# A self-scheduling kernel: longer assumed waits and a fixed seed in its planner, late buffers moved from VectorE to ScalarE, new filler rules, and query stores assumed to land later

## The chip, the cores and the metric

The kernel runs on one core of a Trainium2 chip. A core has TensorE (PE; its weight loads are listed as PEld), VectorE (DVE), ScalarE (ACT), GpSimd (POOL) and SyncE (SP, which issues most transfers here). The metric is the time of one execution in microseconds of device time, as a median of several runs. A span (first to last instruction of a profiled execution) is about 1.8 us shorter than the timed run.

## The reference

Two independent blocks over 2048 rows of width 640, their outputs side by side:

```python
# A: a diagonal complex state-space layer
h[t] = Lam_bar * h[t-1] + B_bar @ x[t]
y[t] = 2 * Re(C @ h[t]) + Dskip * x[t]
# B: attention with 32 heads of 20, one shared key and value head, no mask
q = (x @ wq) split into 32 heads;  k = x @ wk;  v = x @ wv
p = softmax(q k^T / sqrt(20));     out = concat(p v) @ wo
```

The attention makes 32 x 2048 x 2048 scores. The kernel cuts them into 2048 tiles of 128 x 512, and each needs an exponential.

## The kernel before

The kernel does not state an order of instructions. A small event-driven scheduler, which runs while the kernel is built, is given steps with assumed durations and priorities and picks, engine by engine, what goes next. What it picks is emitted as five fixed instruction streams with the semaphore waits that the data needs. The durations in it are assumptions; on the chip only the order counts.

Most score tiles have their exponential on ScalarE, two or three at a time out of a slot of PSUM banks. The others go to VectorE, which makes an approximation by integer arithmetic on the bits of a bf16 (a first pass, then three shifted copies, which GpSimd shares). How many go to VectorE is bounded by `SHARE`, but is decided by what is free at the moment:

```python
OUT = {"pe": 200.0, "act": 130.0, "dve": 110.0, "pool": 150.0, "dma": 60.0}   # ns until a result is seen elsewhere
...
def fill(self, op, i):                       # one ScalarE slot: scores of 2 or 3 tiles, then the exponential
    ...
    ex = self.act(lambda e: e.activation(dst, t[:, 0:512 * n], ACT.Exp, scale=1.0 / UNIT),
                  0.8333 * 512 * n + 64, table="exp", deps=[op], ...)
...
def want_d(self, taken=0, own=0):            # may a tile go to VectorE?
    if self.tile_n >= NTILE - self.LAST or self.d_count + taken + own + 1 > self.SHARE * (self.tile_n - 16):
        return False
    if len(self.d_banks()) <= taken or self.behind():
        return False
    return len(self.d_free()) > taken + own + len(self.SHIFTS) - 1
...
def planned(self):                           # before: the best of 24 seeds by the plan's own end
    for seed in range(self.PLANS):
        ...
        end = max(op.end for op in plan.s.order)
```

The seed moves the due times of background tasks (projections, the state-space layer, output products) by a few tiles, so each seed gives another order, and also another number of tiles on VectorE. Filler products multiply zeros on TensorE and are meant to keep its clock up (in the trace of before it was halved for 6.83 us after 3.41 us in which TensorE was busy for 2.40; that fillers prevent this is not shown by itself in any run here): one source before the first value product (`warm_source`), another after it (`keep_source`).

Of the kernel before, what the change touches and what calls it, by code (L numbers as in the profile page):

```python
# [22 lines left out]
class Op:  # L23


    __slots__ = ("eng", "fns", "dur", "deps", "prio", "reads", "writes", "prev", "gate", "hook", "start", "end",
                 "seq", "land", "dma_key", "idx", "tail", "mode", "load", "late", "port", "after", "due", "table", "psum")

    def __init__(self, eng, fns, dur, deps=(), prio=5, reads=(), writes=(), prev=None, gate=None, hook=None,
                 dma_key=None, land=0.0, tail=0.0, mode="F", load=0.0, port=False):  # L30
        self.eng, self.fns, self.dur = eng, list(fns), dur
        self.deps, self.prio, self.prev = list(deps), prio, prev
        self.reads, self.writes = list(reads), list(writes)
        self.gate, self.hook = gate, hook
        self.dma_key, self.land, self.tail = dma_key, land, tail
        self.mode, self.load, self.late = mode, load, False
        self.port, self.after, self.due, self.table = port, [], None, None
        self.psum = any(k[0] == "B" and k[1:].isdigit() for k in self.reads)
        self.start = self.end = None
        self.seq = self.idx = 0  # L40


class Schedule:
# [5 lines left out]
    ENGINES = ("pe", "act", "dve", "pool", "sp")  # L49
    OUT = {"pe": 200.0, "act": 130.0, "dve": 110.0, "pool": 150.0, "dma": 60.0}  # L50
    OWN = {"pe": 0.0, "act": 60.0, "dve": 115.0, "pool": 100.0}
# [10 lines left out]
    def __init__(self, seed=0):  # L62
# [16 lines left out]
        self.port_wanted = False  # L79
        self.pipe, self.table = 0.0, None  # L80

    def recent(self, span):
# [45 lines left out]
    def begin(self, op, eng):  # L128
# [5 lines left out]
        if eng == "pe":  # L134
            if op.mode != self.mode:
                op.dur += self.SWITCH
                self.mode = op.mode
            self.loads.append((self.t, op.load))
        if op.port:
            if eng == "pool" and self.port_last["dve"] is not None:  # L140
                op.after.append(self.port_last["dve"])
            self.port_free[eng] = self.t + op.dur + (self.LOCK if eng == "pool" else 0.0)
            self.port_last[eng] = op
            self.at(self.port_free[eng])
        if op.dma_key is not None:
            self.free[eng] = self.t + op.tail * len(op.fns)
            s = max(self.t + 1300.0, self.dma_free.get(eng, 0.0), self.pipe)
            self.dma_free[eng] = self.pipe = s + op.dur
# [8 lines left out]
        self.at(self.free[eng])  # L157
        for lag in (0.0, 60.0, 100.0, 110.0, 115.0, 130.0, 150.0, 200.0):
            self.at(op.end + lag)

    stay = staticmethod(lambda: True)
# [244 lines left out]
S, D, NC, H, DH = 2048, 640, 5, 32, 20  # L406
# [8 lines left out]
class Build:  # L415
# [5 lines left out]
    NDS = 20  # L421
    MORE = 21
    SHARE = 0.265
# [15 lines left out]
    def build(self):  # L439
        nc = self.nc  # L440
        with ExitStack() as o:
# [10 lines left out]
            with ExitStack() as p2:  # L452
# [11 lines left out]
                shares.update({f"CT{tb}_{c}": [f"xn{tb}"] for tb in range(2) for c in range(NC)})  # L464
                shares.update({f"DR{self.NDS + i}": over for i, over in enumerate(self.dr_over)})
                shares["WOt"] = [f"BT{i}_{c}" for i in range(2) for c in range(NC)]
                shares.update({f"OPT{k}": [f"BA{i}_{c}" for i in range(2) for c in range(NC)] for k in self.EARLY_O})
# [20 lines left out]

    SPREAD = 12.0
    PLANS = 24  # L490

    def planned(self):

        best = None
        for seed in range(self.PLANS):
            plan = copy.copy(self)
            plan.s = Schedule(seed)
            plan.program()
            try:
                plan.s.run()  # L500
            except RuntimeError:
                continue
            end = max(op.end for op in plan.s.order)
            if best is None or end < best[0]:
# [3 lines left out]
    def alloc(self, o):  # L508
# [9 lines left out]
        for c in range(NC):  # L518
            for m in range(2):
                self.dr_at.append(2048 * c + 640 + 512 * m)  # L520
                self.dr_over.append([f"xbT{i}_{c}" for i in (1, 2, 3)])
        for m in range(6):
            self.dr_at.append(ends[0] + 512 * m)
            self.dr_over.append(["wqa", "wqb"])
        for m in range(NC):
            self.dr_at.append(ends[1] + 512 * m)
            self.dr_over.append([f"QP{m}"])
        self.xaT = sb(o, "xaT", [128, NC, 2, 512], BF16)
# [126 lines left out]
    def program(self):  # L655
# [11 lines left out]
        self.state_op = {}  # L667
        self.owner = [None] * self.NPT
        self.pr_at = 0
# [30 lines left out]
    def warm_source(self):  # L700
# [4 lines left out]
        if self.started:  # L705
            if self.s.recent(3000.0) > self.WARM:
                return None
            fns = self.four(self.pvbank, [p.VZ[:]] * 4, p.KT[:, 0:512], True, True)
            return Op("pe", fns, self.mmt(512), prio=3.5, mode="C", load=512.0, reads=["VZ", "KT0"], writes=[self.pvbank.key],
                      deps=[self.c_op["VZ"], self.kt_op[0]])  # L710
        return Op("pe", [self.mm(self.pvbank.ap, p.PR[:, 0, 0:128], p.PR[:, 0, :], True, True)], 260.0, prio=9,
                  load=512.0, deps=[self.zero_op], reads=["PR0"], writes=[self.pvbank.key], hook=self.warm_last)

    WARM = 4500.0
    V_AT, BOUND_AT = (-88, -87), -99


    KEEP = 3500.0

    def keep_source(self):  # L720
# [6 lines left out]
        if self.s.recent(3000.0) > self.KEEP:  # L727
            return None
        p = self
        bank = self.pvbank  # L730
# [249 lines left out]
    def bound_task(self, m, bank):  # L980
# [3 lines left out]
        for blk in range(NC):  # L984
            prev = self.pe([lambda e, blk=blk: e.matmul(bank.cols(blk, blk + 1), lhsT=p.pick[:, 128 * blk:128 * blk + 128],
                                                        rhs=p.mab[0:DH, 4:5], start=True, stop=True)], 250.0, mode="F", load=8.0,
                           deps=[m, self.c_op["pick"]] + bank.last, prev=prev, prio=1.5, reads=["pick", "mabs"], writes=[bank.key])
        col = bass.AP(tensor=bank.tensor, offset=bank.off, ap=[[bank.tensor.shape[1], 128], [1, NC], [0, 32]])
# [43 lines left out]
    def q_task(self, qb, blk, bank):  # L1032
# [3 lines left out]
        for c in range(NC):  # L1036
# [7 lines left out]
        out = self.dma(lambda e: e.dma_start(rows, dst), 131072, f"qd{blk}", deps=[ev], reads=[key], writes=[f"qd{qb}_{blk}"], prio=0,  # L1044
                       land=300.0)
        self.qd_op[qb, blk] = out
# [137 lines left out]
    def fill(self, op, i):  # L1184
# [17 lines left out]
        for x, m in enumerate(tiles):  # L1202
            b, kc, j = self.score(op, m, t[:, 512 * x:512 * x + 512], banks[x])
            ents.append((b, kc, j, p.PR[:, h.index + x, :]))
        first = [] if own is None else [self.fill_d(op, own, banks[2])]
# [10 lines left out]
        op.load = 128.0 * len(op.fns)  # L1216
        dst = p.PR[:, h.index:h.index + n, :]
        ex = self.act(lambda e: e.activation(dst, t[:, 0:512 * n], ACT.Exp, scale=1.0 / UNIT),  # L1218
# [36 lines left out]
    def pr_next(self, n):  # L1255
        return self.pr_at if self.pr_at + n <= self.NPT else 0

# [173 lines left out]
    def more(self):  # L1431

        yield lambda: NQB - 1 in self.row_mm and self.s.done([self.row_mm[NQB - 1]]) \
            and all(self.s.done([self.qd_op[NQB - 1, i]]) for i in range(NC))
        self.dhold += [Holder(self.NDS + i) for i in range(self.MORE)]

    def d_free(self):
# [866 lines left out]
```

## Time and profile before

| | before |
|---|---|
| median of 3 runs | 745.29 us (744.67 to 746.3) |
| span of the profiled run | 743.5 us |
| ScalarE busy | 97% |
| first exponential starts, last ends | 23.0, 734.4 us |
| exponentials of 1024 and of 1536 columns | 475, 201 |
| score tiles on ScalarE, on VectorE | 1553, 495 |

An exponential over 1024 columns is two tiles, one over 1536 is three. The prediction shows the lines themselves. Read the group rows with care: in "busy, mean ns | idle before" the mean is that of single records, and the records of successive exponentials overlap: in this profile one over 1024 columns has a mean of 1112 ns, and ends 917 ns after the one before it.

### The profile page before, as it was taken

The page shows a single profiled execution, that of the slowest core. Times are in us where ns is not written, and L with a number is a line of the kernel's source. Part 1 is how long each engine was busy: PE and PEld are TensorE (multiplying, and loading weights), DVE is VectorE, ACT ScalarE, POOL GpSimd, SP SyncE. Part 2 cuts the span into 40 slices and gives each one's busy share as a digit, 9 for nine tenths or more (in the row PEclk, how much of TensorE's full clock was granted, in tenths as well). Part 3 has the DMA queues.
Part 4 walks back from the last instruction along what each step waited for, and adds up shares of the span by engine and source line. Part 5 has one row for each costly group of instructions (what it writes and reads, how often), then busy time and mean ns, then how long its engine had stood idle before and what let it go on. Part 6 is the DMA issues. An engine that isn't in the chain of part 4 may idle for free.

```text
span 743.5 us, 26647 instructions
## 1 busy us (share of the span) xinstructions
PE 711.7 (96%) x11323; PEld 255.9 (34%) x11323; DVE 665.3 (89%) x1367; ACT 722.9 (97%) x702; POOL 426.3 (57%) x448
## 2 busy tenths in 40 slices
PE   9999899998999999999999999989999999999997
PEld 3422222234443533332333333323333333332332
DVE  6888999989788798999898999998998998988995
ACT  5999999999999999999999999999999999999995
POOL 3766566430266558367476674566754835778460
PEclk9999999999999999999999999998999999999999
DMA  9414443364220100101100000110000011100101
GB/s 200 70 41 129 91 113 90 89 144 78 48 60 10 25 20 21 51 11 35 42 26 23 17 30 19 40 46 19 19 14 19 9 27 30 37 16 17 26 14 37
DMA packets 78089, 34.43 MB, mean 46 GB/s; under 512 B 58852, under 2 KB 77972, under 8 KB 77972
## 3 DMA queue, kind: packets, MB, share of 16 engines
q1 hardware_dynamic: 76352, 32.34, 18.3%
q8 instruction: 90, 1.47, 0.8%
q10 hardware_dynamic: 1620, 0.39, 0.3%
q14 instruction: 27, 0.22, 0.1%
HBM read 11.53 MB, written 9.75 MB: 29 GB/s over the span
## 4 chain that ended last, share of the span: by engine, by line
ACT 59%; PE 34%; DVE 6%; issue 1%; DVEq 0%
ACT PR L1218 59%; PE MB L637 12%; PE SC L637 11%; PE MB L633 10%; DVE BIG L652 2%; DVE prod L647 1%; DVE W L652 1%; DVE CT L647 1%; DVE CA L647 1%; DVE g L2046 0%; PE SC L633 0%; DVE pvsb L1580 0%; DVE CT L651 0%; DVE CA L651 0%; PE SC L935 0%
## 5 line engine op out<-in xcount | busy, mean ns | idle before, releaser
L1218 ACT ACTIVATE PR<-SC 128x1024 bf16<-128x1024 f32 (+1 forms) x676 | 708.6, 1252 | 3.3 <-PE SC L637 2.1
L647 POOL TENSOR_TENSOR BIG<-BIG,step 128x512 int32<-128x512 int32 x401 | 407.4, 1045 | 286.1 <-DVE BIG L652 163.1
L652 DVE TENSOR_SCALAR BIG<-SC 128x512 int16<-128x512 f32 x456 | 302.8, 684 | 38.5 <-PE SC L637 34.9
L637 PE MATMUL SC<-QT,KT 32*128 32x512 bf16 x2009 | 265.3, 386 | 23.0 <-ACT PR L1218 16.0
L637 PE MATMUL MB<-BIG,VS 128*32 128x512 bf16 x1980 | 248.5, 386 | 1.2 <-issue 0.6
L637 PE MATMUL MB<-PR,VP 128*32 128x512 bf16 x1553 | 217.4, 386 | 0.8 <-DVE pvsb L1580 0.6
L637 PEld LDWEIGHTS SC<-QT,KT 32*128 32x128 bf16 x2009 | 67.8, 91 | 258.2 <-ACT PR L1218 165.3
L652 DVE TENSOR_SCALAR BIG<-BIG 128x1024 int16<-128x1024 int16 (+1 forms) x356 | 129.0, 419 | 8.6 <-PE MB L637 7.0
L637 PEld LDWEIGHTS MB<-BIG,VS 128*32 128x32 bf16 x1980 | 62.6, 95 | 66.7 <-issue 44.1
L637 PEld LDWEIGHTS MB<-PR,VP 128*32 128x32 bf16 x1553 | 53.5, 94 | 54.6 <-issue 41.0
L633 PE MATMUL MB<-CT,W 128*32 128x320 bf16 (+2 forms) x1040 | 49.7, 301 | 0.2 <-DVE BIG L2006 0.2
L633 PE MATMUL MB<-xaT,BT 128*32 128x256 bf16 x800 | 34.5, 274 | 0.0
L633 PE MATMUL MB<-xaT,BA 128*32 128x256 bf16 x800 | 33.6, 274 | 0.1
L633 PE MATMUL MB<-CA,W 128*32 128x512 bf16 (+1 forms) x640 | 31.2, 301 | 0.1
L647 DVE TENSOR_TENSOR prod<-MB,tab 128x1024 bf16<-128x1024 f32 x20 | 24.3, 1215 | 3.7 <-PE MB L633 3.7
L652 DVE TENSOR_SCALAR BIG<-MB 128x512 int16<-128x512 f32 x39 | 26.5, 680 | 1.1 <-PE MB L637 0.7
L633 PEld LDWEIGHTS MB<-CT,W 128*32 128x32 bf16 x1040 | 21.4, 96 | 17.0 <-issue 7.9
L633 PE MATMUL MB<-WO,OP 128*32 128x128 bf16 (+1 forms) x576 | 26.5, 297 | 0.1
L1761 DVE CAST stg<-MB 128x512 bf16<-128x512 f32 x35 | 23.9, 683 | 2.6 <-PE MB L633 2.3
L633 PE MATMUL MB<-BIG 128*32 128x512 bf16 x340 | 25.6, 383 | 0.0
L2046 DVE TENSOR_TENSOR_SCAN g<-sc,hst,prod 128x256 bf16<-128x256 f32 x30 | 23.1, 776 | 0.0
L633 PEld LDWEIGHTS MB<-xaT,BA 128*32 128x32 bf16 x800 | 19.0, 96 | 9.0 <-issue 5.4
(167 smaller groups left out, 421.2 us busy)
## 6 DMA issues: line engine op xcount, KB each, us to landing
out_dram<-stg SPq DMA_DIRECT2D x31, 128.0 KB, 1.7
qd<-BIG SPq DMA_DIRECT2D x20, 128.0 KB, 1.8
QT<-qd SPq DMA_DIRECT2D x28, 80.0 KB
OP<-pvsb SPq DMA_DIRECT2D x105, 20.0 KB
rdP<-recs SPq DMA_DIRECT2D x105, 20.0 KB
W<-in_A_B_re_dram SPq DMA_DIRECT2D x10, 160.0 KB, 2.7
W<-in_A_B_im_dram SPq DMA_DIRECT2D x10, 160.0 KB, 2.7
lbd<-W SPq DMA_DIRECT2D x10, 160.0 KB, 2.0
```

What stands on the lines that cost most here:

```text
L633: r = e.matmul(out[32 * j:32 * j + 32], lhsT=lhsT[:, 32 * j:32 * j + 32], rhs=rhs, start=start, stop=stop, tile_position=(0, 32 * j), skip ...
L637: return lambda e: e.matmul(out, lhsT=lhsT, rhs=rhs, start=start, stop=stop, **kw)
L647: return lambda e: e.tensor_tensor(out, a, b, op)
L652: return lambda e: e.tensor_scalar(out, a, s1, s2, op0=op0, op1=op1)
L1218: ex = self.act(lambda e: e.activation(dst, t[:, 0:512 * n], ACT.Exp, scale=1.0 / UNIT), 0.8333 * 512 * n + 64, table="exp", deps=[op], re ...
L1761: ev = self.dve(lambda e: e.tensor_copy(st, bank.ap), 645, deps=[prev], reads=[bank.key], writes=[key], prio=self.EV, gate=(lambda: last.e ...
L2046: o = self.dve(lambda e, ri=ri, init=init: e.tensor_tensor_scan(p.g[:, u, ri, :], rdec, p.prod[:, 1, 0, ri, :], init, ALU.mult, ALU.add), ...
```

## The change

The intent, as the code reads: make the plan agree with the chip. Steps are lengthened by the waits that will be emitted, a finished plan is replayed with all of these waits and penalised for stretches of low TensorE activity, one seed that scores well is fixed, fillers become urgent when activity is low, and late buffers are shared out differently.

```diff
-    OUT = {"pe": 200.0, "act": 130.0, ...}
+    OUT = {"pe": 200.0, "act": 225.0, ...}
+    SEEN = {"pe": 215.0, "act": 225.0, ...}          # for the replay
 ...
+        wait = self.stall(op)                        # waits for all readers and writers of its buffers
+        if wait > 0.0:
+            if op.dma_key is None:
+                op.dur += wait
+                op.stall = wait
 ...
+    def replayed(self): ...                          # end of the replay + self.gated(work)
+    WINDOW, IDLE, RANGE, COST = 3413.0, 2700.0, 700.0, 1500.0
 ...
-    MORE = 21                                        # more VectorE tile buffers, late in the kernel
+    MORE = 10
 ...
-    PLANS = 24
+    SEEDS = (198,)
-            end = max(op.end for op in plan.s.order)
+            end = plan.s.replayed()
 ...
+        self.wide_at = [(self.NPT, 6, ends[0]), (self.NPT + 6, NC, ends[1])]   # 11 buffers to ScalarE instead
 ...
+            low = self.s.mode != "S" and self.s.recent(2800.0) < self.LOW
-            return Op("pe", fns, ..., prio=3.5, ...)                 # warm_source
+            return Op("pe", fns, ..., prio=0.3 if low else 2.5, ...)
-    WARM = 4500.0
+    WARM = 3500.0
 ...
+        low = self.s.mode != "S" and self.s.recent(2800.0) < self.LOW   # keep_source: computed, not used
         return Op("pe", fns, self.mmt(256, 4), prio=8, ...)
 ...
-                       land=300.0)
+                       land=4000.0 if qb > 1 else 300.0)              # query stores
```

Left out: the code of the replay, the addressing of the shared buffers, warm-up durations of 240 instead of 260 ns, the priority 0.5 instead of 1.5 of five small products that make the score bound, and the seed's spread of due times, 8 tiles instead of 12 (`SPREAD`). The constants of the score are its author's assumptions; of its clock constants only the 3413 ns has a counterpart in the traces here, the 3.41 us steps told of below.

More of the change, by code (lines that the diff above doesn't have):

```diff
@@ L26 @@
     __slots__ = ("eng", "fns", "dur", "deps", "prio", "reads", "writes", "prev", "gate", "hook", "start", "end",
-                 "seq", "land", "dma_key", "idx", "tail", "mode", "load", "late", "port", "after", "due", "table", "psum")
+                 "seq", "land", "dma_key", "idx", "tail", "mode", "load", "late", "port", "after", "due", "table", "psum", "stall", "found")
     def __init__(self, eng, fns, dur, deps=(), prio=5, reads=(), writes=(), prev=None, gate=None, hook=None,
@@ L39, in __init__ @@
         self.start = self.end = None
+        self.stall = 0.0
         self.seq = self.idx = 0
@@ L49 @@
     ENGINES = ("pe", "act", "dve", "pool", "sp")
-    OUT = {"pe": 200.0, "act": 130.0, "dve": 110.0, "pool": 150.0, "dma": 60.0}
+    OUT = {"pe": 200.0, "act": 225.0, "dve": 110.0, "pool": 150.0, "dma": 60.0}
+    SEEN = {"pe": 215.0, "act": 225.0, "dve": 110.0, "pool": 150.0, "dma": 60.0}
     OWN = {"pe": 0.0, "act": 60.0, "dve": 115.0, "pool": 100.0}
@@ L80, in __init__, with stall @@
         self.pipe, self.table = 0.0, None
+        self.writer, self.readers = {}, {}
+    def stall(self, op):
+        eng, late = op.eng, self.t
+        found = list(op.after)
+        for k in op.reads:
+            if k in self.writer:
+                found.append(self.writer[k])
+            if k[0] == "B" and k[1:].isdigit():
+                found += [x for x in self.readers.get(k, ()) if x.eng != eng]
+        for k in op.writes:
+            if k in self.writer:
+                found.append(self.writer[k])
+            found += self.readers.get(k, ())
+        op.found = [d for d in found if d is not op and (eng != "pe" or d.eng != "pe")]
+        for d in op.found:
+            late = max(late, self.seen(d, eng))
+        for k in op.reads:
+            self.readers.setdefault(k, []).append(op)
+        for k in op.writes:
+            self.writer[k] = op
+            self.readers[k] = []
+        return late - self.t
     def recent(self, span):
@@ L138, in begin @@
             self.loads.append((self.t, op.load))
+        if op.port and eng == "pool" and self.port_last["dve"] is not None:
+            op.after.append(self.port_last["dve"])
+        wait = self.stall(op)
[3 more added lines that the diff above has]
+                op.stall = wait
         if op.port:
-            if eng == "pool" and self.port_last["dve"] is not None:
-                op.after.append(self.port_last["dve"])
             self.port_free[eng] = self.t + op.dur + (self.LOCK if eng == "pool" else 0.0)
@@ L145, in begin @@
         if op.dma_key is not None:
-            self.free[eng] = self.t + op.tail * len(op.fns)
-            s = max(self.t + 1300.0, self.dma_free.get(eng, 0.0), self.pipe)
+            self.free[eng] = self.t + wait + op.tail * len(op.fns)
+            s = max(self.t + wait + 1300.0, self.dma_free.get(eng, 0.0), self.pipe)
             self.dma_free[eng] = self.pipe = s + op.dur
@@ L157, in begin, with replayed, gated @@
         self.at(self.free[eng])
-        for lag in (0.0, 60.0, 100.0, 110.0, 115.0, 130.0, 150.0, 200.0):
+        for lag in (0.0, 60.0, 100.0, 110.0, 115.0, 150.0, 200.0, 225.0):
             self.at(op.end + lag)
+    def replayed(self):
+        free = {e: 0.0 for e in self.ENGINES}
+        port = {"dve": 0.0, "pool": 0.0}
+        end, queue, work = {}, 0.0, []
+        for op in self.order:
+            e = op.eng
+            t = free[e]
+            for d in op.found:
+                out = self.SEEN["dma"] if d.dma_key is not None else self.OWN.get(e, 0.0) if d.eng == e else self.SEEN[d.eng]
+                t = max(t, end[id(d)] + out)
+            dur = op.dur - op.stall
+            if op.port:
+                t = max(t, port["pool" if e == "dve" else "dve"])
+                port[e] = t + dur + (self.LOCK if e == "pool" else 0.0)
+            if op.dma_key is not None:
+                free[e] = t + op.tail * len(op.fns)
+                queue = max(t + 1300.0, queue) + dur
+                end[id(op)] = max(queue + 700.0, free[e] + 1700.0) + op.land
+            else:
+                end[id(op)] = t + dur + op.tail
+                free[e] = t + dur - (self.EARLIER.get(e, 0.0) if op.psum else 0.0)
+                if e == "pe" and t > 14000.0:
+                    work.append((t, op.load))
+        return max(end.values()) + self.gated(work)
+    WINDOW, IDLE, RANGE, COST = 3413.0, 2700.0, 700.0, 1500.0
+    def gated(self, work):
+        low, lo, total = [], 0, 0.0
+        for t, w in work[:-40]:
+            total += w
+            while work[lo][0] < t - self.WINDOW:
+                total -= work[lo][1]
+                lo += 1
+            if total - w < self.IDLE and t - work[0][0] > self.WINDOW:
+                if low and t - low[-1][0] < 2 * self.WINDOW:
+                    low[-1][1] = min(low[-1][1], total - w)
+                else:
+                    low.append([t, total - w])
+        return sum(self.COST * min(1.0, (self.IDLE - v) / self.RANGE) for t, v in low)
     stay = staticmethod(lambda: True)
@@ L465, in build @@
                 shares.update({f"DR{self.NDS + i}": over for i, over in enumerate(self.dr_over)})
+                shares.update({f"PR{self.NPT + i}": over for i, over in enumerate(self.pr_over)})
                 shares["WOt"] = [f"BT{i}_{c}" for i in range(2) for c in range(NC)]
@@ L487, in lay_banks @@
         self.early = [b for b in self.banks if b not in rest]
-    SPREAD = 12.0
-    PLANS = 24
+    SPREAD = 8.0
+    SEEDS = (198,)
     def planned(self):
         best = None
-        for seed in range(self.PLANS):
+        for seed in self.SEEDS:
             plan = copy.copy(self)
@@ L521, in alloc @@
                 self.dr_over.append([f"xbT{i}_{c}" for i in (1, 2, 3)])
-        for m in range(6):
-            self.dr_at.append(ends[0] + 512 * m)
-            self.dr_over.append(["wqa", "wqb"])
-        for m in range(NC):
-            self.dr_at.append(ends[1] + 512 * m)
-            self.dr_over.append([f"QP{m}"])
+        self.wide_at = [(self.NPT, 6, ends[0]), (self.NPT + 6, NC, ends[1])]
+        self.pr_over = [["wqa", "wqb"]] * 6 + [[f"QP{m}"] for m in range(NC)]
         self.xaT = sb(o, "xaT", [128, NC, 2, 512], BF16)
@@ L667, in program @@
         self.state_op = {}
-        self.owner = [None] * self.NPT
+        self.owner = [None] * (self.NPT + len(self.pr_over))
+        self.wide = False
         self.pr_at = 0
@@ L707, in warm_source @@
                 return None
+            low = self.s.mode != "S" and self.s.recent(2800.0) < self.LOW
             fns = self.four(self.pvbank, [p.VZ[:]] * 4, p.KT[:, 0:512], True, True)
-            return Op("pe", fns, self.mmt(512), prio=3.5, mode="C", load=512.0, reads=["VZ", "KT0"], writes=[self.pvbank.key],
+            return Op("pe", fns, self.mmt(512), prio=0.3 if low else 2.5, mode="C", load=512.0, reads=["VZ", "KT0"], writes=[self.pvbank.key],
                       deps=[self.c_op["VZ"], self.kt_op[0]])
-        return Op("pe", [self.mm(self.pvbank.ap, p.PR[:, 0, 0:128], p.PR[:, 0, :], True, True)], 260.0, prio=9,
+        return Op("pe", [self.mm(self.pvbank.ap, p.PR[:, 0, 0:128], p.PR[:, 0, :], True, True)], self.COLD if self.s.t < self.WARMED else 240.0, prio=9,
                   load=512.0, deps=[self.zero_op], reads=["PR0"], writes=[self.pvbank.key], hook=self.warm_last)
-    WARM = 4500.0
+    COLD, WARMED = 240.0, 6000.0
+    WARM = 3500.0
     V_AT, BOUND_AT = (-88, -87), -99
     KEEP = 3500.0
+    LOW = 2400.0
     def keep_source(self):
@@ L986, in bound_task @@
                                                         rhs=p.mab[0:DH, 4:5], start=True, stop=True)], 250.0, mode="F", load=8.0,
-                           deps=[m, self.c_op["pick"]] + bank.last, prev=prev, prio=1.5, reads=["pick", "mabs"], writes=[bank.key])
+                           deps=[m, self.c_op["pick"]] + bank.last, prev=prev, prio=0.5, reads=["pick", "mabs"], writes=[bank.key])
         col = bass.AP(tensor=bank.tensor, offset=bank.off, ap=[[bank.tensor.shape[1], 128], [1, NC], [0, 32]])
@@ L1203, in fill @@
             b, kc, j = self.score(op, m, t[:, 512 * x:512 * x + 512], banks[x])
-            ents.append((b, kc, j, p.PR[:, h.index + x, :]))
+            ents.append((b, kc, j, self.pr(h.index + x, 1)[:, 0, :]))
         first = [] if own is None else [self.fill_d(op, own, banks[2])]
@@ L1216, in fill @@
         op.load = 128.0 * len(op.fns)
-        dst = p.PR[:, h.index:h.index + n, :]
+        dst = self.pr(h.index, n)
         ex = self.act(lambda e: e.activation(dst, t[:, 0:512 * n], ACT.Exp, scale=1.0 / UNIT),
@@ L1255, in pr_next, with pr @@
     def pr_next(self, n):
-        return self.pr_at if self.pr_at + n <= self.NPT else 0
+        ends = [self.NPT] + ([at + k for at, k, _ in self.wide_at] if self.wide else [])
+        end = next((e for e in ends if e > self.pr_at), None)
+        if end is None:
+            return 0
+        if self.pr_at + n <= end:
+            return self.pr_at
+        return end if end < ends[-1] else 0
+    def pr(self, i, n):
+        for at, k, base in self.wide_at:
+            if at <= i < at + k:
+                lo = base + 512 * (i - at)
+                return self.BIG[:, lo:lo + 512 * n].rearrange("p (i n) -> p i n", n=512)
+        return self.PR[:, i:i + n, :]
     def tight(self):
@@ L1435, in more @@
         self.dhold += [Holder(self.NDS + i) for i in range(self.MORE)]
+        self.wide = True
     def d_free(self):
```

## The prediction

One paragraph is cut out of the prediction. No term of its sum rested on it: 745.3 + 3.0 - 1.2 - 1.4 - 0.3 - 0.6 = 744.8 us.

> **What bounds the kernel now.** I read the busy shares first. Four engines look full, so a share alone does not name the bound. Here are the page's busy shares, two of its slice rows, its first line of the last chain, and its first group.
>
> ```profile
> PE 711.7 (96%) x11323; PEld 255.9 (34%) x11323; DVE 665.3 (89%) x1367; ACT 722.9 (97%) x702; POOL 426.3 (57%) x448
> ...
> ACT  5999999999999999999999999999999999999995
> ...
> PEclk9999999999999999999999999998999999999999
> ...
> ACT 59%; PE 34%; DVE 6%; issue 1%; DVEq 0%
> ...
> L1218 ACT ACTIVATE PR<-SC 128x1024 bf16<-128x1024 f32 (+1 forms) x676 | 708.6, 1252 | 3.3 <-PE SC L637 2.1
> ```
>
> The last row decides it: the exponentials of the softmax occupy ScalarE for 708.6 us of a 743.5 us span and were made to wait only 3.3 us. TensorE and VectorE are idle by choice of the plan, ScalarE is not. I then split the group by shape, because its 1252 ns is a mixture.
>
> ```profile
> L1218 ACT ACTIVATE PR<-SC 128x1024 bf16<-128x1024 f32 x475 | 447.9, 1112 | 2.0 <-PE SC L637 1.4
> L1218 ACT ACTIVATE PR<-SC 128x1536 bf16<-128x1536 f32 x201 | 277.9, 1585 | 1.3 <-PE SC L637 0.7 <-PE MB L637 0.4
> ```
>
> The means of single records are too long to multiply: neighbouring records overlap (447.9 + 277.9 = 725.8, but their union is 708.6). What counts is the distance from one end to the next. Over the single records I find a median of 917 ns for a 1024 and 1344 ns for a 1536; the undisturbed ones scatter by one or two ns, so I use 916.5 and 1343.5. This shows what "idle" hides: a delay of up to some 0.2 us is swallowed by the overlap. The timeline of ScalarE gives the ends of the stretch (start, length, group, idle before).
>
> ```profile
> 22.23 0.20 ACT L1855 ACTIVATE tload<-tload 128x1 f32<-128x1 f32 x1
> 23.02 13.86 ACT L1218 ACTIVATE PR<-SC 128x1024 bf16<-128x1024 f32 x15 [0.58 <-PE SC L637]
> ...
> 724.33 10.10 ACT L1218 ACTIVATE PR<-SC 128x1024 bf16<-128x1024 f32 x8
> 734.93 0.38 ACT L1585 ACTIVATE pvsb<-MB 128x256 bf16<-128x256 f32 x1 [0.51 <-PE MB L637]
> ```
>
> So the run is 23.0 us of start, 711.4 us of exponentials (to 734.42), 9.1 us of end, and 1.8 us between span (743.5) and timed run (745.3). Pure work is 475 x 0.9165 + 201 x 1.3435 = 705.4 us; summing each distance's excess over its form gives 5.9 us of stall. That 5.9 us is all a better order can win in the middle. The largest piece is in the stretch where the clock row shows its 8:
>
> ```profile
> 500.00:502.00 2.00, 1.45 (x17) 0.41 (x17) 2.00 (x5) 2.00 (x3) 2.00 (x3) 1.00 0.19 44
> 502.00:504.00 2.00, 2.00 (x18) 0.41 (x18) 2.00 (x4) 2.00 (x3) 2.00 (x3) 0.62 0.17 40
> 504.00:506.00 2.00, 2.00 (x19) 0.46 (x19) 1.37 (x3) 1.45 (x3) 1.61 (x2) 0.50 0.08 21
> 506.00:508.00 2.00, 2.00 (x19) 0.25 (x12) 2.00 (x5) 1.51 (x2) 1.04 (x1) 0.50 0.08 16
> 508.00:510.00 2.00, 2.00 (x22) 0.46 (x22) 0.86 (x4) 1.94 (x2) 0.00 (x0) 0.68 0.19 41
> ```
>
> (Columns: length, then busy us of PE, weight loads, DVE, ACT, POOL, then clock, DMA share, GB/s.) TensorE was 1.22 us busy in 498 to 500 and 1.45 in 500 to 502; then its clock halved for 6.8 us, the score products came late, and ScalarE idled 0.55 + 0.49 + 0.06 = 1.10 us, 1.6 us with the hidden delays there.
>
> [...]
>
> **The change part by part.** The planner runs while the kernel is built, so none of its Python costs chip time; only the emitted order counts. It now (a) lengthens each planned step by semaphore waits it used not to plan, takes ScalarE results to be visible 225 ns after the end instead of 130, and scores a plan by a replay plus a penalty for low TensorE activity; (b) takes one seed, 198, instead of the best of 24; (c) gives late in the kernel 11 freed 128x512 buffers to ScalarE's exponentials and only 10, not 21, to VectorE's tiles; (d) assumes query stores of the last two blocks to land 3.7 us later; (e) alters fillers. Comparing the emitted orders gives these counts.
>
> ScalarE: 475 + 201 exponentials become 446 of 1024 (341 into the old tile, 105 into the freed space) and 223 of 1536 (174 + 49). In 512-column tiles 1553 becomes 1561; VectorE's share falls from 495 to 487. Pure work: 446 x 0.9165 + 223 x 1.3435 = 708.4 us, **+3.0 us on the path that sets the end**. The wider form saves some: a tile costs 0.448 us in threes and 0.458 in pairs; without it eight tiles would be +3.6.
>
> VectorE and GpSimd: eight fewer first passes (8 x 0.68 us), 12 more double copies (x 0.36), 16 more single ones (x 0.21), so about +2 us on VectorE; GpSimd has 32 fewer copies (x 1.05 = 33 us less). Both lie beside ScalarE and count zero unless they cause a stall.
>
> TensorE: 11323 products become about 11310, and changes between score products and the others 1319 runs to 1309. Zero.
>
> Fillers: the 256-column ones go 356 to 360, the 512-column ones 16 to 20. The intent "high priority when activity is low" reaches only the warm-up source, used before the first value product: in the other source the variable is computed and never used, its priority stays 8. So whatever prevents a dip after the start is the choice of seed, not the priority. I value the dip at -1.6 us and expect it gone, since the new score punishes such a stretch: **-1.2 us** with a 75% chance.
>
> Remaining stall: 5.9 - 1.6 = 4.3 us. Planned waits and a replay-chosen seed should take some; I take a third, **-1.4 us**. This is the choice with least behind it. More exponential buffers win nothing: exponentials waited 0.4 us on value products in the whole run.
>
> Start: ScalarE's order differs only in where the key evictions stand among the table steps; TensorE has two more warm-up products of about 0.22 us amid its serial transposes, and the maximum's five small products come sooner. I put it at 0, give or take 0.4. End: the last value products now run in 28 instructions after the last score pair instead of 40, and the final ScalarE eviction no longer stands behind eight extra output products (about 0.4 us), but VectorE's three additions of 0.68 us still end within 0.3 us of it: **-0.3 us**. Query stores: 0; the waits of TensorE name no transfer.
>
> Sum: 745.3 + 3.0 - 1.2 - 1.4 - 0.3 = 745.4. A fixed seed was presumably kept because it ran well, which the trace cannot show; for that I take another 0.6 us off: **744.8 us**.
>
> **Rivals.** (1) The plan becomes nearly free of stalls. For it: it was picked on a replay with all waits. Then 23.0 + 708.4 + 8.8 + 1.8 = 742.0 us; hardly anything can be lower, because ScalarE's work itself has grown. (2) Planned waits do not match the chip (ScalarE to TensorE is now taken at 225 ns), fewer VectorE buffers delay block ends, and stalls stay or a new dip appears: 745.3 + 3.0 + 1 = 749 us. For it: the two largest single delays before, 0.60 us each, come from such a dip, so one more costs 1.6. (3) TensorE becomes the bound, being 96% busy. Against it: its records overlap and its product count does not rise; it waited 16.0 us for ScalarE itself. It would need several dips.
>
> **Range and chances.** The floor of 742.0 and the rival of 749 enclose the plausible; I take 741.8 to 748.2. Two per cent is 14.9 us: faster than 730.4 is below the floor of ScalarE's work, slower than 760.2 needs about nine dips. Faster 0.01, same 0.98, slower 0.01.
>
> **What would show it.** In the new profile: exponentials 446 + 223, their union near 711 to 713; ends still 917 and 1344 ns apart; the first at 22.6 to 23.4 us; 8.5 to 9.1 us after the last; stall 2 to 5 us; no clock slice below 9 in the middle. A first exponential a microsecond earlier, a shorter per-form distance, or a stall above 7 us would prove a step wrong.

## The result, and the profile after

The changed kernel took 747.79 us in the median (747.64 to 748.77, 4 runs), the kernel before 745.64 us in the same rounds (the three runs of the table above and a fourth). The ratio is 1.0033, with a 95% interval of 1.0015 to 1.005. Ratios here are the mean time of one kernel's fast runs over that of the other's fast runs of the same rounds, so they are not quite the ratio of the medians. It is a small loss, well within 2%. It lies inside the predicted range of 741.8 to 748.2, but only by 0.4 us, and the centre of 744.8 was 3.0 us too low: the prediction put the change at half a microsecond of gain, and it was a loss of 2.2 us.

The page of the changed kernel, the same lines as in the prediction (the exponentials now have two rows, because some write into freed space of another tile):

```profile
PE 709.5 (95%) x11310; PEld 256.7 (34%) x11310; DVE 659.4 (88%) x1387; ACT 726.0 (97%) x695; POOL 393.6 (53%) x416
...
ACT  5899999999999999999999999999999999999995
...
ACT 60%; PE 34%; DVE 4%; issue 1%; SPq 1%; DMA 0%; DVEq 0%
...
L1294 ACT ACTIVATE PR<-SC 128x1024 bf16<-128x1024 f32 (+1 forms) x515 | 555.5, 1264 | 3.3 <-PE SC L708 3.1
...
L1294 ACT ACTIVATE BIG<-SC 128x1024 bf16<-128x1024 f32 (+1 forms) x154 | 171.1, 1263 | 0.5 <-PE SC L708 0.2
```

ScalarE is still the engine that never rests, and the only one with more work: 726.0 us against 722.9. VectorE, GpSimd and TensorE all do a little less. The groups by shape, and the timeline of ScalarE at both ends:

```profile
L1294 ACT ACTIVATE PR<-SC 128x1024 bf16<-128x1024 f32 x341 | 324.8, 1100 | 3.2 <-PE SC L708 3.1
L1294 ACT ACTIVATE PR<-SC 128x1536 bf16<-128x1536 f32 x174 | 243.4, 1585 | 0.1
L1294 ACT ACTIVATE BIG<-SC 128x1024 bf16<-128x1024 f32 x105 | 104.1, 1111 | 0.5 <-PE SC L708 0.2
L1294 ACT ACTIVATE BIG<-SC 128x1536 bf16<-128x1536 f32 x49 | 71.3, 1590 | 0.0
```

```profile
23.09 5.61 ACT L1294 ACTIVATE PR<-SC 128x1024 bf16<-128x1024 f32 x6 [0.80 <-PE SC L708]
29.43 1.02 ACT L1294 ACTIVATE PR<-SC 128x1024 bf16<-128x1024 f32 x1 [0.74 <-PE SC L708]
...
732.52 5.22 ACT L1294 ACTIVATE BIG<-SC 128x1536 bf16<-128x1536 f32 x4
738.27 0.39 ACT L1675 ACTIVATE pvsb<-MB 128x256 bf16<-128x256 f32 x1 [0.54 <-PE MB L708]
```

There are 341 + 105 = 446 and 174 + 49 = 223 exponentials, and the ends of successive ones are still 917 and 1343 ns apart in the median (before, too; the prediction read 1344). The two forms differ by 427 ns for 512 columns, 0.834 ns a column, which leaves 62.5 ns to each exponential beside its columns. The pure work is therefore the 708.4 us of the prediction. The run of exponentials goes from 23.09 to 737.73 us. With pure work as before worked out, the two profiled spans divide so (stall is the excess of each end-to-end distance over 916.5 or 1343.5 ns, summed; the columns are 0.1 us short of the span, because the first exponential has nothing to overlap with and takes 1.02 us):

| us | before | changed | changed, second profile |
|---|---|---|---|
| start, to the first exponential | 23.02 | 23.09 | 22.51 |
| pure work of the exponentials | 705.4 | 708.4 | 708.4 |
| stall among them | 5.91 | 6.18 | 5.35 |
| of it in the first 95 us | 0.03 | 1.63 | 0.87 |
| of it from 190 to 285 us | 0.50 | 1.58 | 1.42 |
| of it from 475 to 570 us, where the old dip was | 1.88 | 0.28 | 0.37 |
| of it after 665 us | 0.11 | 0.94 | 0.94 |
| end, after the last exponential | 9.08 | 9.30 | 9.31 |
| span | 743.5 | 747.0 | 745.6 |

Almost the whole difference of the spans, 3.5 us in the first pair, is the 3.0 us of exponential work. The stall did not go away; it moved. The idle time before the exponentials is smaller, 3.3 us before and 3.8 us after in the rows above; the rest of the 5.91 and 6.18 us is seen only in the distances between ends. The stretch of the old dip won 1.5 us, and the start, the stretch from 190 us and the last 80 us lost more than that between them, at nearly the same places in both profiles. Of the 17 delays over 0.1 us in the second profile, 15 are exponentials that began within 0.05 us of the end of their last score product: they waited for score products that came late, although the clock was full there. At the start, in the first profile, the clock halved as well (columns as in the prediction: length, busy us of PE, weight loads, DVE, ACT, POOL, then clock, DMA share, GB/s):

```profile
24.00:28.00 4.00, 3.39 (x32) 1.76 (x36) 3.18 (x17) 4.00 (x6) 3.61 (x9) 0.88 0.47 105
28.00:32.00 4.00, 4.00 (x38) 0.86 (x30) 3.22 (x9) 2.68 (x4) 3.47 (x8) 0.70 0.20 45
```

ScalarE lost 1.32 of the 4 us from 28 to 32. This run was the slowest of the four (748.77 us at a mean clock of 0.996; the others, 747.64 to 747.81 us, had 0.999 or 1.0).

### The profile page after: what moved, and what is told of

Read it like the earlier page. It is cut to its first block, busy times and chain, and to the rows that moved or that the text cites. A ratio compares the mean times of both kernels' runs of the same rounds, so it can differ in the third digit from the quotient of the medians.

```text
span 747.0 us, 26533 instructions
## 1 busy us (share of the span) xinstructions
PE 709.5 (95%) x11310; PEld 256.7 (34%) x11310; DVE 659.4 (88%) x1387; ACT 726.0 (97%) x695; POOL 393.6 (53%) x416
## 4 chain that ended last, share of the span: by engine, by line
ACT 60%; PE 34%; DVE 4%; issue 1%; SPq 1%; DMA 0%; DVEq 0%
ACT PR L1294 48%; PE MB L704 12%; ACT BIG L1294 12%; PE SC L708 11%; PE MB L708 10%; DVE prod L718 1%; DVE BIG L723 1%; SPq L1724 0%; DMA W<-in_A_B_im_dram 0%; PE SC L704 0%; DVE mab L965 0%; DVE PR L718 0%; DVE pvsb L1670 0%; DVE W L723 0%; DVE CT L718 0%
## 5 line engine op out<-in xcount | busy, mean ns | idle before, releaser
L1294 ACT ACTIVATE PR<-SC 128x1024 bf16<-128x1024 f32 (+1 forms) x515 | 555.5, 1264 | 3.3 <-PE SC L708 3.1
L718 POOL TENSOR_TENSOR BIG<-BIG,step 128x512 int32<-128x512 int32 x369 | 374.7, 1047 | 321.4 <-DVE BIG L723 199.5
L723 DVE TENSOR_SCALAR BIG<-SC 128x512 int16<-128x512 f32 x422 | 280.2, 683 | 38.6 <-PE SC L708 33.1
L708 PE MATMUL MB<-BIG,VS 128*32 128x512 bf16 x1948 | 211.8, 383 | 0.9 <-DVE BIG L723 0.5
L1294 ACT ACTIVATE BIG<-SC 128x1024 bf16<-128x1024 f32 (+1 forms) x154 | 171.1, 1263 | 0.5 <-PE SC L708 0.2
L708 PE MATMUL MB<-PR,VP 128*32 128x512 bf16 x1204 | 153.6, 384 | 0.3
L708 PE MATMUL MB<-BIG,VP 128*32 128x512 bf16 x357 | 56.3, 384 | 0.0
L708 PEld LDWEIGHTS MB<-PR,VP 128*32 128x32 bf16 x1204 | 39.3, 94 | 40.7 <-issue 27.4
L723 DVE TENSOR_SCALAR BIG<-MB 128x512 int16<-128x512 f32 x65 | 44.1, 678 | 0.7 <-PE MB L708 0.6
L708 PE MATMUL MB<-QT,KT 32*128 32x512 bf16 x65 | 25.0, 384 | 0.2 <-DVE BIG L1118 0.2
```

What stands on the lines that cost most here:

```text
L708: return lambda e: e.matmul(out, lhsT=lhsT, rhs=rhs, start=start, stop=stop, **kw)
L718: return lambda e: e.tensor_tensor(out, a, b, op)
L723: return lambda e: e.tensor_scalar(out, a, s1, s2, op0=op0, op1=op1)
```

## The experiments

All twelve were correct. There were three calls, each on one chip with eleven runs of the kernel before; the medians of these were 744.43, 744.82 and 744.57 us. The changed kernel was repeated in the second call only, so a difference from its 747.34 us crosses calls, with some 0.4 us of doubt, unless the text says "of the same call". "Stall" and the like are from the one profiled run of each, which need not be the median run: the two profiles of the changed kernel differ by 0.8 us of stall. The times are medians of 4 to 6 runs.

| kernel | us | ratio to before | exponentials | pure work | us less pure work | stall | first 95 us |
|---|---|---|---|---|---|---|---|
| before | 744.4 to 744.8 | 1 | 475 + 201 | 705.4 | 39.0 to 39.4 | 5.9 | 0.0 |
| changed, again | 747.34 | 1.0028 | 446 + 223 | 708.4 | 38.9 | 5.4 | 0.9 |
| smaller share on VectorE | 759.29 | 1.0200 | 415 + 252 | 718.9 | 40.4 | 5.8 | 1.4 |
| old buffers | 747.24 | 1.0043 | 464 + 209 + 1 | 706.5 | 40.7 | 6.0 | 0.9 |
| old buffers, seed 25 | 746.41 | 1.0025 | 465 + 209 + 1 | 707.5 | 39.0 | 7.4 | 2.7 |
| no planned waits | 749.49 | 1.0065 | 456 + 218 | 710.8 | 38.7 | 4.6 | 0.9 |
| 130 ns again | 749.72 | 1.0071 | 455 + 219 | 711.2 | 38.5 | 3.0 | 0.2 |
| old fillers | 752.57 | 1.0093 | 448 + 222 | 708.8 | 43.7 | 9.6 | 4.3 |
| filler priority completed | 750.90 | 1.0083 | 456 + 218 + 1 | 711.3 | 39.6 | 4.7 | 1.5 |
| seed 6 | 754.18 | 1.0118 | 443 + 227 | 711.0 | 43.2 | 10.0 | 4.3 |
| all undone, seed 198 | 744.68 | 1.0002 | 476 + 201 | 706.3 | 38.4 | 3.7 | 0.0 |
| all undone, seed 158 | 743.74 | 0.9987 | 477 + 199 | 704.5 | 39.2 | 4.7 | 0.0 |
| all undone, seed 1185 | 742.41 | 0.9971 | 484 + 193 + 1 | 703.4 | 39.0 | 5.4 | 0.0 |

The "+ 1" is a last exponential of a single tile (512 columns), which four of the orders have; it ends 490 ns after the one before it. The expectations of these four were written without it, so their pure work is 0.5 us too low.

**The changed kernel again**, unchanged.

> The changed kernel once more, unchanged, so that the others of this call have it on the same chip. Ratio to before 1.003 again, first exponential near 23 us, stall 4.5 to 6.5 us; if the clock dip after 27 us was chance, most runs are without it, at a clock of 0.999 or 1.

It came out at 747.05 to 747.82 us in six runs, with clocks of 0.998 to 1.0. The dip at 27 us comes in some executions and not in others: the second profile has none, with the same order and as little work before that moment (TensorE is busy for 2.40 us from 24.00 to 27.01 us in both profiles). These are the second profile's rows:

```profile
24.00:28.00 4.00, 3.38 (x41) 1.43 (x45) 3.21 (x15) 4.00 (x6) 3.61 (x9) 1.00 0.50 105
28.00:32.00 4.00, 3.28 (x45) 0.89 (x37) 3.46 (x9) 3.53 (x5) 3.41 (x9) 1.00 0.20 44
```

Busy time alone does not tell when a dip comes. Here are 3.41 us before and 3.41 us after the clock fell in the first profile of the changed kernel, the 3.41 us before it fell in the kernel before, and an emptier stretch of the experiment with the completed filler priority, after which it did not fall (columns: length, busy us of PE, clock, DMA share, GB/s):

```profile
23.60:27.02 3.42, 2.81 (x32) 1.00 0.51 115
27.02:30.43 3.41, 3.41 (x28) 0.50 0.34 77
499.05:502.46 3.41, 2.40 (x28) 1.00 0.23 57
187.84:191.25 3.41, 1.87 (x38) 1.00 0.00 0
```

Idle gaps do not tell it either: TensorE's longest was 0.41 us in the first of these stretches and 0.60 us in the third, and 0.95 us in the last one, where the clock stayed at 1.00. In the first profiles of the two kernels the clock changes only at whole steps of 3.41 us from its first record (20.48 us, six steps, to the dip at 27.02), and the halved stretches among the exponentials lasted one and two such steps (3.41 us in the changed kernel, 6.83 us before). Why it falls in one execution of the same order and not in another is not shown. The start is a weak place of the new orders all the same: five of the ten profiles of the changed kernel and its variants have a halved clock that begins between 25.8 and 29.2 us, and none of the four of the planner of before.

**Raising the suspected cost.** More exponentials for ScalarE, less for everybody else.

```diff
-    SHARE = 0.265
+    SHARE = 0.23
```

> The changed kernel with VectorE's share of the score tiles capped lower (0.23 instead of 0.265): 462 tiles on VectorE instead of 487, exponentials 415 of 1024 and 252 of 1536, pure work 415 x 0.9165 + 252 x 1.3435 = 718.9 us against 708.4. Theory A (ScalarE's own work sets the time, stalls stay where they were): +10.5 us, about 758.3 us. Rival B (the order of the plan and its stalls set it, ScalarE's work is partly hidden): under +5 us, since VectorE and TensorE get less to do.

```profile
L1294 ACT ACTIVATE PR<-SC 128x1024 bf16<-128x1024 f32 x325 | 317.5, 1110 | 2.4 <-PE SC L708 2.0
L1294 ACT ACTIVATE PR<-SC 128x1536 bf16<-128x1536 f32 x190 | 271.2, 1583 | 0.2
L1294 ACT ACTIVATE BIG<-SC 128x1024 bf16<-128x1024 f32 x90 | 90.3, 1139 | 0.7 <-PE SC L708 0.7
L1294 ACT ACTIVATE BIG<-SC 128x1536 bf16<-128x1536 f32 x62 | 90.2, 1602 | 0.0
```

The rows show 325 + 90 = 415 and 190 + 62 = 252. The median is 12.0 us above the changed kernel's (759.29 - 747.34) for 10.5 us more pure work. Nothing of the work is hidden, and rival B falls. Relief of VectorE and TensorE gave nothing back; the time grew by 1.5 us more than the work. The program's verdict at 2% is "unclear" (the ratio's interval is 1.0187 to 1.0213), but the loss itself is far outside the noise.

**The buffers returned to VectorE**, at the same seed and at a seed chosen for that layout.

```diff
-    MORE = 10
+    MORE = 21
-        self.wide_at = [(self.NPT, 6, ends[0]), (self.NPT + 6, NC, ends[1])]
+        self.wide_at, self.pr_over = [], []        # and the 11 addresses back into dr_at
```

> The changed kernel with the 11 freed buffers given back to VectorE's tiles (21 of them late instead of 10), seed 198: 492 tiles on VectorE, exponentials 464 + 209, pure work 706.0 us, 2.4 less than changed. Theory A: about 745.4 us. Rival B (the extra exponential buffers spared stalls that come back): 747.5 us or more, with a stall well above 6.2 us in the trace.

> The changed kernel with the 11 freed buffers given back to VectorE's tiles, and a seed (25) picked for that layout: 465 + 209 exponentials, pure work 707.0 us, 1.4 less than changed. Theory A: 745.9 us. Rival B (the extra exponential buffers spare stalls): 747.3 us or more, as the same layout with seed 198 gave, where chosen and unchosen seeds were compared.

VectorE got 492 tiles instead of 487, so at seed 198 these buffers are where five of the tiles went. But theory A was wrong there by nearly 2 us (1.3 with the single tile counted): 747.24 us, with runs from 746.18 to 750.51 and clocks of 0.992 to 0.999, the changed kernel's time for 1.8 us less work. Rival B's stall did not appear in the trace either (5.95 us), but that trace is of the quickest of the six runs, so where the median run lost its time is not shown. Seed 198 had been chosen for the other layout. With seed 25 (490 tiles) the median is 746.41 us: 0.9 us less than the changed kernel for 0.9 us less work. Its profiled run, the slowest (748.59 us), had a halved clock of 6.8 us near the start. So the pure work explains the second of these two and not the first.

**Without the planned waits.**

```diff
         wait = self.stall(op)
+        wait = 0.0
```

> The changed kernel without the planned waits (225 ns and all else kept), seed 198: 456 + 218 exponentials, pure work 710.8 us, 2.4 more than changed. Theory A (the planned waits spare no stall; ScalarE's work sets the time): +2.4 us on the changed kernel, stall in its trace 4 to 6.5 us. Rival D (planned waits do spare stalls, and the change lost only through its fewer VectorE tiles): stall of 8 us or more, +5 us or more. The new score rates this plan 9.7 us worse.

It was 2.15 us above the changed kernel of the same call (749.49 - 747.34), and its stall was 4.57 us, not 8. Theory A holds, rival D falls: at this seed the planned waits spared no stall that can be seen. They did leave VectorE with more tiles than this variant (487 against 482), which was not their purpose.

**The old visibility of ScalarE's results in the plan.**

```diff
-    OUT = {"pe": 200.0, "act": 225.0, ...}
+    OUT = {"pe": 200.0, "act": 130.0, ...}
```

> The changed kernel with ScalarE's results taken to be visible to the plan after 130 ns again instead of 225 (the replay keeps 225), seed 198: 455 + 219 exponentials, pure work 711.2 us, 2.8 more than changed. Theory A: +2.8 us, about 750.1 us. Rival G (130 ns is nearer to the chip, so its plan stalls less): 748.5 us or less, stall under 4 us in the trace.

Each theory had one number right. The stall of the profiled run was the least of all, 3.04 us, as rival G said; the time, 749.72 us, is theory A's, since the order gives ScalarE 2.8 us more work. But the profiled run (748.21 us) was one of the quickest, 1.5 us under the median. Three runs were at 748.2 to 748.5 us, the others at 751.0 to 754.4 us, two of them with clocks of 0.994 and 0.989. So no help of the longer assumed delay against stalls is seen.

**The old fillers.**

```diff
-    ... prio=0.3 if low else 2.5      WARM = 3500.0      (small products) prio=0.5
+    ... prio=3.5                      WARM = 4500.0      (small products) prio=1.5
```

> The changed kernel with the old fillers (warm-up threshold 4500, priority 3.5, 260 ns, the five small products of the bound late again), seed 198: 448 + 222 exponentials, pure work 708.8 us. Theory E (the new fillers let the clock dip after the start): no halved clock between 25 and 32 us in any profile, and a few tenths to 1 us faster. Rival: no difference beyond 0.5 us, the dip of the first profile was chance.

Theory E fell, and in the opposite direction: 5.2 us slower than the changed kernel (752.57 - 747.34), with 4.3 us of stall in the first 95 us. The windows show a clock at half for 10.2 us:

```profile
28.00:32.00 4.00, 3.93 (x42) 1.31 (x45) 3.65 (x15) 3.80 (x5) 3.46 (x8) 0.65 0.28 62
32.00:36.00 4.00, 4.00 (x32) 0.59 (x24) 1.81 (x4) 2.40 (x3) 1.22 (x3) 0.50 0.03 12
36.00:40.00 4.00, 4.00 (x36) 0.77 (x33) 1.98 (x3) 2.37 (x3) 2.03 (x2) 0.57 0.16 54
```

TensorE reads "4.00 of 4.00" in the last two rows and is yet the cause, since busy time does not show the halved clock: at half clock it makes about 34 products where the changed kernel's second profile has 56 and 57, and ScalarE is left with 2.4 of 4 us. At seed 198 the new plan needs the new fillers. Whether it is their priority or the other order that comes with them is not separated: seed 6 below has the new fillers, and the same 4.3 us of stall beside the same 10.2 us of halved clock. They are no gain over the kernel before, which had 0.03 us of stall there without them.

**The intent of the fillers completed** in the second source.

```diff
-        return Op("pe", fns, self.mmt(256, 4), prio=8, ...)
+        return Op("pe", fns, self.mmt(256, 4), prio=0.3 if low else 8, ...)
```

> The changed kernel with its intent finished: the second filler source, too, gets priority 0.3 when recent TensorE activity is low (its variable was computed and not used), seed 198: 456 + 218 exponentials, pure work 710.8 us, 2.4 more. Theory A: +2.4 us, about 749.7 us, whatever the clock does after the start. Rival F (the unused priority is where the gain went): at or under the changed kernel's time, clock 1.0 in every run.

Rival F falls: 750.90 us, clocks of 0.995 to 0.999. That is 3.6 us above the changed kernel, 2.9 of it exponential work (with the single tile) and 0.7 unexplained. The unused variable cost nothing here.

**Another seed in the changed planner**, which its own score rates worse.

```diff
-    SEEDS = (198,)
+    SEEDS = (6,)
```

> The changed kernel with seed 6 instead of 198: 443 + 227 exponentials, pure work 711.0 us, 2.6 more. Theory A: +2.6 us, give or take 1. Rival C (the score ranks plans of one planner rightly, it only fails between planners): the score says +4.2 us. A result near 0 would say neither.

It was 6.8 us slower than the changed kernel of the same call, more than either expected. Pure work gives 2.6 us; the rest is stall, 10.04 us in the profile, of which 4.32 us lie in the first 95 us beside a halved clock of 10.2 us. Between these two seeds of one planner the score had the right sign.

**Everything undone but the fixed seed**, and two other seeds of the old planner.

```diff
 # old buffers, no planned waits, 130 ns, land=300.0, old fillers, and:
     SEEDS = (198,)      # then (158,) and (1185,), these with SPREAD = 12.0
```

> Every part of the change undone except the fixed seed: old buffers, no planned waits, ScalarE visible at 130 ns, old landing time, old fillers, seed 198 with its smaller spread. Exponentials 476 + 201, pure work 706.3 us. Theory A: near the kernel before plus 0.9, 745.5 to 747. Rival C (the new score is right about plans): the score rates this plan 9.6 us worse than the changed one, so about 757 us.

> The planner of before with another seed (158, spread 12), picked because ScalarE's pure work is the least of 160 seeds: 477 + 199 exponentials, 704.5 us, VectorE 497 tiles; the new score rates it 4.7 us worse than the changed kernel. Theory A: 744 to 745.5 us, faster than both. Rival C: 750 us or more.

> The planner of before (all parts undone) with seed 1185, picked from some 1350 seeds for a short plan and little exponential work: 484 + 193 exponentials, pure work 702.9 us, 2.5 less than before, 500 tiles on VectorE. Theory A: 742 to 743 us, faster than before, changed and seed 158. Rival: the tighter plan stalls by as much as it saves, 743.7 us or more. The new score rates it 749.4.

All three are level with the kernel before or below it: 744.68, 743.74 and 742.41 us. Rival C falls outright: the plans that the new score rated 9.6 and 4.7 us worse than the changed kernel's ran 2.7 and 3.6 us faster (seeds 198 and 158), and the one that it rated at 749.4 us took 742.41. Theory A's ranges were missed on the good side by seeds 198 (0.8 us) and 158 (0.3 us), whose profiles have 2.2 and 1.2 us less stall than that of the kernel before: work is most of the time, but stalls don't quite stay as they are. Seed 1185 met its range. It is faster than both kernels, at 0.9971 of before with an interval of 0.9948 to 0.9994 (within 2%), and mainly by the means that theory A names:

```profile
L1300 ACT ACTIVATE PR<-SC 128x1024 bf16<-128x1024 f32 x484 | 456.2, 1109 | 2.6 <-PE SC L714 1.9 <-PE MB L714 0.2
L1300 ACT ACTIVATE PR<-SC 128x1536 bf16<-128x1536 f32 x193 | 266.9, 1593 | 0.4 <-PE MB L714 0.4
```

Its stall, 5.42 us, is within 0.5 us of that of the kernel before (5.91). It has 500 tiles on VectorE and, with its single tile, 2.0 us less exponential work; its median is 2.2 us lower (744.57 - 742.41).

## Why the prediction was right or wrong

**The bound: right.** In every kernel ScalarE is filled from the first exponential to the last. In the table, time less pure work stays between 38.4 and 40.7 us, but for the two kernels with the longest halved clock at the start (43.2 and 43.7), while pure work ranges over 15.5 us.

**"+3.0 us on the path that sets the end": right, and nearly the whole result.** The counts, the distances of 917 and 1343 ns and the sum were met, and the change in the median was 2.2 and 2.5 us in the two calls that had both kernels. Raising the cost by 10.5 us more, in the smaller share, confirmed that it is paid in full.

**The engines beside ScalarE: counted zero, rightly.** The side estimate of 2 us more for VectorE (0.36 and 0.21 us for a double and a single copy; back to back, their ends are 0.335 and 0.202 us apart in the trace of before) was off, its busy time fell by 5.9 us (665.3 to 659.4), and GpSimd's by 32.7; neither bought time.

**The dip, "-1.2 us": right where it looked, not in the sum.** The new plan avoids the dip at 502 us: from 475 to 570 us the stall fell from 1.88 to 0.28 and 0.37 us, and the changed kernel's clocks in its second call are 0.998 to 1.0, where those of the kernel before are 0.988 to 1.0 with a median of 0.997. But the changed kernel's first profile had its own dip of 3.4 us at the start. The prediction looked for dips where the old kernel had one and not where the new order lets the clock fall.

**The remaining stall, "-1.4 us": failed.** This is the mis-sized term that the prediction named as having the least behind it, and the step with the largest error. Outside the old dip's stretch (475 to 570 us) the stall rose from 4.0 us to 5.9 and 5.0 us instead of falling by a third; in all it was 6.18 and 5.35 us where 2.9 was expected. Two runs speak against the step itself: without planned waits the stall was 4.57 us, with 130 ns it was 3.04 us, each in one profile. Planning the waits did not reduce the stall in any run here.

**Start, 0 give or take 0.4: about right for the first exponential** (23.09 us; 22.51 us in the second profile, 0.1 us outside), but the step ended there. In the first 95 us the changed kernel stalls by 0.9 to 1.6 us, most of it within 10 us of the first exponential, where the old one has 0.03 us. Calling the fillers' priority irrelevant after the start was right; treating them as worth zero was not, because at seed 198 the new plan loses 5.2 us when they go back, though part of that may be the order that changes with them.

**End, "-0.3 us": the sign failed; it was +0.2 us.** The timeline of the second profile shows what the order did:

```profile
737.05 1.05 PE L704 MATMUL SC<-WO,OP 128*32 128x512 bf16 x16
737.92 0.27 PE L704 MATMUL SC<-E,pvsb 128*32 128x4 bf16 x16
...
741.19 0.68 DVE L718 TENSOR_TENSOR PR<-SC,BA 128x512 bf16<-128x512 f32 x1
```

and before:

```profile
735.82 0.26 PE L633 MATMUL SC<-E,pvsb 128*32 128x4 bf16 x16 [0.30 <-DVE pvsb L1587]
...
739.07 0.68 DVE L647 TENSOR_TENSOR PR<-SC,BA 128x512 bf16<-128x512 f32 x1
```

Sixteen output products now stand ahead of the small denominators (E). Counted from the first eviction of the last value product (736.86 and 734.93 us), these start after 1.06 us instead of 0.89, and VectorE's last addition after 4.33 us instead of 4.14. The prediction counted products saved behind the denominators and overlooked those moved ahead of them.

**The 0.6 us for a seed that was "presumably kept because it ran well": not borne out.** It was a guess about the author and not a reading of the profile. Seed 198 does run 6.8 us better than the one other seed tried in the changed planner, so the seed may be a good one of its planner; what it is worth against a usual seed stays open. No gain over the kernel before came of it: the same seed in the old planner ran 2.7 us faster than in the new one (744.68 against 747.34 us).

**Rivals.** No run of the changed plan came near the floor of 742.0 us of the first rival. TensorE as the lasting bound did not appear. What was nearest to the truth is rival 2, in part: stalls stay, and dips come in some runs. That the result still fell into the stated range is partly luck: the work term was right, the savings set against it were not there in sum, and the range was wide enough by 0.4 us.

So where did the expected gain go? Exponential work grew by the 3.0 us foreseen, and the 3.5 us that were to pay for it (dip, stall, end, seed) were mostly not there: what the old dip gave back was lost at other places. Why VectorE gets fewer tiles is settled only in part: at seed 198 the old buffers restore five and undoing everything six, but undoing the planned waits or the 225 ns alone takes away five or six more, so the parts do not add up one by one. The later landing of the query stores and the smaller spread of the seed were not tried alone. Why the score misranks plans of the two planners stays open: no run here tests one of its assumed delays by itself.

## What to carry to other kernels

When one engine is full from end to end, first count what a change adds to that engine's own work; here eight more tiles, 3.0 us of exponentials, outweighed every refinement of the order. A plan's score is worth what its ranking on the chip is worth: test it on plans of both planners before letting it choose. Seeds and small order changes move such a kernel by several microseconds (742.41 to 744.68 us over three seeds of the old planner here, 747.34 and 754.18 us with two of the new), so undo a part at more than one seed before crediting or blaming it.
